# Attention with a low-rank mixer on one core: k transposed first in the first pair, and uT of the fourth pair in two PSUM banks

## The chip, the cores and the metric

One core of a Trainium2 chip. The metric is the device time of one execution in microseconds. A run of a program on one core is called slow when it is over 1.5% above the fastest of the same kernel. The granted clock is the share of full speed that TensorE was given in a stretch. PSUM is the memory in which this kernel keeps the tiles that TensorE writes its products to, SBUF that of the tiles it reads them from. By a bank is meant here a part of 512 columns of the kernel's PSUM tiles: an accumulator tile has one, a score tile two. The span of a profile is some 1.8 us shorter than the time of the same execution: 408.0 us of span went with 409.81 us of time.

## The reference, cut to what matters

Eight batches of attention with 8 heads, 576 positions and 64 channels per head, with a bias by relative position, and behind it a mixer: a low-rank product over the positions (U, V) is added to x, which gives u, and u goes through two dense layers (w1, w2).

```python
scores = scale * np.matmul(q, k.transpose(0, 1, 3, 2)) + bias      # softmax, times v -> x
xt = x.transpose(0, 2, 1)
h = xt @ U @ V
u = x + h.transpose(0, 2, 1)
ch = np.maximum(u @ w_ch1, 0.0) @ w_ch2
return u + ch
```

## The kernel before: the parts that matter here

Heads are handled in pairs; batch 0 has pairs 0 to 3, numbered on through the batches. The first pair's q and k are transposed on TensorE into two PSUM tiles; VectorE copies q's, ScalarE copies k's:

```python
def first_transposes(pr, srcs, copies):          # pr = 0: srcs = (q, k), copies = (vector, scalar)
    # ... tv[0], tv[1]: one PSUM tile each
    for ti, src in enumerate(srcs):
        for t in range(4):
            if pr == 0:
                nc.tensor.transpose(tv[ti][:, t], src[:, t * 128 : (t + 1) * 128], ident)
            # ...
    for ti in range(2):
        copies[ti](out=qkT[0][:, pr, ti, 0:S0]..., in_=tv[ti]...)
```

u transposed (uT) is what w1 is multiplied with. For the pairs of batch 0 TensorE makes it, in one PSUM tile of the pool `acc` (three tiles of one bank); tt is the low-rank part, copied to SBUF by ScalarE just before:

```python
def mix_ut(g, copy):
    tp = acc()
    nc.tensor.matmul(tp, lhsT=tt, rhs=vpad[:, 0:S0], start=True, stop=False, ...)
    for t in range(4):
        nc.tensor.matmul(tp[:, t * 128 : (t + 1) * 128], lhsT=x[:, t, :], rhs=ident, ...)
    copy(uT[b % 3][:, pr, :], tp)

# ... at the end of batch 0's attention
mix_t(3, nc.scalar.copy)                 # tt of the fourth pair
mix_ut(3, nc.vector.tensor_copy)         # uT of the fourth pair; the first w1 products follow
```

The scores come from another pool, `sc`, of two tiles with two banks each. GpSimd issues most loads on one queue. For batch 2 they come in this order, and TensorE transposes the four q tiles of pair 8 at about 70 us:

```python
for t in range(NKT):                     # NKT = 4
    for which in range(2):               # q, k
        seq.append(lambda which=which, t=t: main(which, t))
```

And at the start, GpSimd waits for the small bias table in DRAM (gp_dram) before it loads v of batch 0:

```python
nc.gpsimd.dma_start(out=gate, in_=gp_dram[0:1, 0:2])
load_rem(0, 2)                           # v, last 64 rows
for t in range(NKT):
    load_main(0, 2, t)                   # v, four tiles
```

The softmax here doesn't subtract the row's maximum and nothing guards it: scores larger than these inputs give would overflow.

## Time and profile before

| | before |
|---|---|
| median of the first three runs | 409.9 us (409.36 to 410.46) |
| span of the profile, mean granted clock | 408.0 us, 0.992 |
| first scores | 7.66 us |
| first uT product of the fourth pair | 38.13 us |
| first w1 product that needs it | 39.53 us |
| transpose of the fourth q tile of pair 8 | 70.68 us, after 1.30 us of waiting |

The chain of waits runs through loads up to the last row of the table and through TensorE from there on. The lines are in the prediction.

### The profile page before, as it was taken

What the parts mean: (1) busy time and instruction counts of PE and PEld (TensorE: products, weight loads), DVE (VectorE), ACT (ScalarE), POOL (GpSimd) and SP (SyncE); (2) the same over time, 40 slices, a digit from 0 to 9 for tenths busy, and PEclk for the clock granted to TensorE, in tenths of its full rate; (3) what the DMA queues carried; (4) which work ended last, traced back from release to release, by engine and by line L of the source; (5) the groups of instructions that cost most, each with busy time, mean ns of one, the idle gap of its engine ahead of it and who ended that gap; (6) DMA issues with size and microseconds to landing.
All of it is one profiled execution on the core that took longest, in us unless ns stands there. A gap on an engine that the chain in (4) does not pass through costs nothing.

```text
span 408.0 us, 9061 instructions
## 1 busy us (share of the span) xinstructions
PE 386.7 (95%) x3636; PEld 214.8 (53%) x3700; DVE 243.2 (60%) x554; ACT 207.0 (51%) x289; POOL 124.7 (31%) x179
## 2 busy tenths in 40 slices
PE   3888998999999999999999999999999999999995
PEld 1456555555555555555555555555555554444443
DVE  6867887757664675566755776568655832422321
ACT  5886644565654566557655665455555640220310
POOL 4948924454454045404540454040000000000000
PEclk9789999999999999999999999999999999999999
DMA  7999999999999599949995999499022003001012
GB/s 130 181 159 157 112 187 128 119 104 155 151 78 117 123 117 94 129 104 135 108 100 130 127 88 91 110 135 105 14 66 66 14 14 95 35 4 75 26 27 77
DMA packets 162754, 40.68 MB, mean 100 GB/s; under 512 B 151792, under 2 KB 157176, under 8 KB 162712
## 3 DMA queue, kind: packets, MB, share of 16 engines
q0 software_dynamic: 108416, 17.97, 62.2%
q1 hardware_dynamic: 53080, 21.22, 25.6%
q10 hardware_dynamic: 1216, 0.92, 0.7%
q8 instruction: 29, 0.48, 0.5%
q14 instruction: 13, 0.11, 0.1%
HBM read 37.84 MB, written 9.45 MB: 116 GB/s over the span
## 4 chain that ended last, share of the span: by engine, by line
PE 81%; DMA 10%; POOL 5%; issue 2%; DVE 1%; ACT 0%; ACTq 0%; POOLq 0%
PE acc L392 30%; PE acc L372 27%; PE o L611 10%; PE sc L524 7%; DMA w1b<-in_moe_w_ch_dram 5%; DMA w2b<-in_moe_w_ch_dram 4%; PE acc L647 2%; POOL v_bf L255 2%; POOL qb L265 1%; PE acc L663 1%; DMA qb<-in_q_dram 1%; PE sc L537 1%; PE sc L558 1%; POOL qb L255 1%; DMA gp_dram<-gp 1%
## 5 line engine op out<-in xcount | busy, mean ns | idle before, releaser
L533 ACT ACTIVATE p_sb<-sc 128x1024 bf16<-128x1024 f32 x128 | 124.6, 1021 | 101.3 <-PE sc L524 101.1
L392 PE MATMUL acc<-w2b,g 128*128 128x512 bf16 (+1 forms) x560 | 128.7, 373 | 2.3 <-DVE ob L401 0.5
L372 PE MATMUL acc<-uT,w1b 128*128 128x512 bf16 x484 | 116.3, 380 | 2.5 <-issue 0.6
L392 PEld LDWEIGHTS <-g 128*128 128x128 bf16 x592 | 55.2, 98 | 70.2 <-issue 11.7
L372 PEld LDWEIGHTS <-w1b 128*128 128x128 bf16 x576 | 53.3, 98 | 71.5 <-issue 13.1
L383 DVE TENSOR_SCALAR g<-acc 128x512 bf16<-128x512 f32 x94 | 64.7, 690 | 34.7 <-PE acc L372 31.7
L587 DVE TENSOR_TENSOR p_sb<-p_sb,eb 128x768 bf16<-128x768 bf16 (+3 forms) x160 | 69.8, 465 | 12.1 <-ACT p_sb L533 9.5
L381 ACT ACTIVATE g<-acc 128x512 bf16<-128x512 f32 x50 | 29.9, 598 | 59.8 <-PE acc L372 59.6
L611 PEld LDWEIGHTS <-p_sb 128*128 128x128 bf16 x1600 | 56.3, 98 | 6.9 <-issue 1.3
L611 PE MATMUL o<-v_bf,p_sb 128*128 128x65 bf16 x1500 | 58.3, 194 | 0.2 <-DVE p_sb L587 0.2
L401 DVE TENSOR_TENSOR ob<-acc,u_tok 128x512 f32<-128x512 f32 x32 | 22.1, 691 | 44.3 <-PE acc L392 39.4
L524 PE MATMUL sc<-qkT 64*128 64x512 bf16 x256 | 41.7, 395 | 1.3 <-ACT qkT L469 0.7
L914 POOL COPY gate<-xp 1x2 bf16<-1x2 bf16 x18 | 3.1, 175 | 121.7 <-DVE xp L636 121.7
L671 DVE TENSOR_TENSOR u_tok<-acc,xp 128x512 bf16<-128x512 f32 x32 | 22.1, 691 | 24.8 <-PE acc L663 24.7
L636 DVE TENSOR_TENSOR xp<-o,rcp 128x320 bf16<-128x320 f32 x60 | 29.5, 491 | 3.2
L255 POOL DMA_DIRECT2D v_bf<-in_v_dram x32 | 28.5, 915 | 2.0 <-DMA w1b<-in_moe_w_ch_dram 1.7
L255 POOL DMA_DIRECT2D qb<-in_q_dram x24 | 22.1, 921 | 5.0 <-DVE p_sb L587 5.0
L255 POOL DMA_DIRECT2D qb<-in_k_dram x24 | 21.9, 910 | 5.5 <-DMA w2b<-in_moe_w_ch_dram 3.5
L567 ACT ACTIVATE p_sb<-sc 128x640 bf16<-128x640 f32 x32 | 22.4, 698 | 0.4 <-PE sc L561 0.3
L550 ACT ACTIVATE p_sb<-sc 128x512 bf16<-128x512 f32 x32 | 19.1, 598 | 3.5 <-PE sc L537 1.2
L634 DVE RECIPROCAL rcp<-o 128x5 f32<-128x5 f32 x60 | 11.5, 191 | 14.0 <-PE o L611 13.3
L647 PEld LDWEIGHTS <-upad 128*128 128x128 bf16 x160 | 11.4, 98 | 7.8 <-DVE xp L636 0.7
(90 smaller groups left out, 257.5 us busy)
## 6 DMA issues: line engine op xcount, KB each, us to landing
out_dram<-ob SPq DMA_DIRECT2D x32, 256.0 KB, 2.3
v_bf<-in_v_dram POOLq DMA_DIRECT2D x32, 128.0 KB, 5.7
qb<-in_q_dram POOLq DMA_DIRECT2D x27, 128.0 KB, 4.4
qb<-in_k_dram POOLq DMA_DIRECT2D x27, 128.0 KB, 4.5
w1b<-in_moe_w_ch_dram POOLq DMA_DIRECT2D x2, 1024.0 KB, 9.3
w2b<-in_moe_w_ch_dram POOLq DMA_DIRECT2D x2, 1024.0 KB, 12.5
stage<-gp_dram SPq DMA_DIRECT2D x4, 192.0 KB, 4.6
qkT<-qb SPq DMA_TRANSPOSE x40, 5.0
```

The lines of the kernel that those rows point to most:

```text
L255: nc.gpsimd.dma_start(out=dst, in_=src[b, :, t * 128 : (t + 1) * 128, :].rearrange("h p d -> p h d"),)
L372: nc.tensor.matmul(gp_, lhsT=w1b[:, ct, nt * 128 : (nt + 1) * 128], rhs=rhs[:, ct, :], start=(ct == 0), stop=(ct == 3),)
L381: nc.scalar.activation(g[:, nt, :], gp_, AF.Relu)
L383: nc.vector.tensor_relu(out=g[:, nt, :], in_=gp_)
L392: nc.tensor.matmul(op[:, c0:c1], lhsT=g[:, nt, tt * 128 : (tt + 1) * 128], rhs=w2b[:, nt, c0:c1], start=(nt == 0), stop=(nt == NHT - 1), s ...
L401: nc.vector.tensor_tensor(out=ob[:, c0:c1].rearrange("p (a c) -> p a c", c=128), in0=op[:, c0:c1].rearrange("p (a c) -> p a c", c=128), in ...
L524: nc.tensor.matmul(sp[:, hh, :], lhsT=kT[rows, i * 128 : (i + 1) * 128], rhs=qT[rows, 0:S0], start=True, stop=True,)
L533: nc.scalar.activation(P[:, i, :, 0:S0], sp, AF.Exp, scale=scale)
L567: nc.scalar.activation(P4[:, 0:SP], sp.rearrange("p a c -> p (a c)")[:, 0:SP], AF.Exp, scale=scale,)
L587: nc.vector.tensor_tensor(out=t, in0=t, in1=e, op=ALU.mult)
L611: nc.tensor.matmul(o[:, qt * 66 : qt * 66 + 65], lhsT=lhs[:, c0 : c0 + 128], rhs=rhs, start=(kt == NKT and qt == 0), stop=(kt == NKT - 1), ...
L636: nc.vector.tensor_tensor(out=xo[:, :, hh], in0=o[:, :, 0:64], in1=rbc, op=ALU.mult)
```

## The change

The intent: let k be transposed as soon as it is cast, since ScalarE casts it before q, and copy uT of the fourth pair with two engines side by side from two banks, since TensorE waits 0.29 us for that copy.

```diff
-        for ti, src in enumerate(srcs):
+        for ti in (1, 0) if pr == 0 else (0, 1):
+            src = srcs[ti]
             for t in range(4):
...
-        for ti in range(2):
+        for ti in (1, 0) if pr == 0 else (0, 1):
             copies[ti](
...
     mix_t(3, nc.scalar.copy)
-    mix_ut(3, nc.vector.tensor_copy)
+    x, tt = x_pr[3], tt_pr[3]
+    sc = ps_s.tile([128, 2, 512], FP32, name="sc")
+    for w, copy in enumerate((nc.scalar.copy, nc.vector.tensor_copy)):
+        cols = slice(w * 256, (w + 1) * 256)
+        nc.tensor.matmul(sc[:, w, 0:256], lhsT=tt, rhs=vpad[:, cols], start=True, ...)
+        for t in range(2):
+            nc.tensor.matmul(sc[:, w, t * 128 : (t + 1) * 128], lhsT=x[:, 2 * w + t, :], rhs=ident, ...)
+        copy(uT[0][:, 3, cols], sc[:, w, 0:256])
```

(The arguments of the two products are shortened.)

More of the change, by code (lines that the diff above doesn't have):

```diff
@@ L889 @@
     mix_t(3, nc.scalar.copy)
-    mix_ut(3, nc.vector.tensor_copy)
+    x, tt = x_pr[3], tt_pr[3]
+    sc = ps_s.tile([128, 2, 512], FP32, name="sc")
+    for w, copy in enumerate((nc.scalar.copy, nc.vector.tensor_copy)):
+        cols = slice(w * 256, (w + 1) * 256)
+        nc.tensor.matmul(
+            sc[:, w, 0:256], lhsT=tt, rhs=vpad[:, cols], start=True, stop=False,
+            skip_group_check=True,
+        )
+        for t in range(2):
+            nc.tensor.matmul(
+                sc[:, w, t * 128 : (t + 1) * 128],
+                lhsT=x[:, 2 * w + t, :],
+                rhs=ident,
+                start=False,
+                stop=(t == 1),
+                skip_group_check=True,
+            )
+        copy(uT[0][:, 3, cols], sc[:, w, 0:256])
     put_off = [lambda g=g: mix_h(g) for g in range(NPAIR)]
```

## The prediction

> **What bounds the kernel now.** I read four views, in this order: the page's chain of work that ended last, the same chain cut to the first 75 us, the waits of TensorE up to 75 us, and the timeline around the two places that the change touches. The page says TensorE: busy 95% of the span, and 81% of the chain. But the change lies in the first 40 us, so what matters is what carries the chain there. That is another thing:
>
> ```profile
> PE 386.7 (95%) x3636; PEld 214.8 (53%) x3700; DVE 243.2 (60%) x554; ACT 207.0 (51%) x289; POOL 124.7 (31%) x179
> PE 81%; DMA 10%; POOL 5%; issue 2%; DVE 1%; ACT 0%; ACTq 0%; POOLq 0%
> ```
>
> ```profile
> 17.48 10.41 DMA w1b<-in_moe_w_ch_dram
> ...
> 29.68 8.12 DMA w1b<-in_moe_w_ch_dram
> ...
> 47.67 14.56 DMA w2b<-in_moe_w_ch_dram
> 62.24 0.30 issue
> 62.54 2.59 POOL qb L255 x3
> 65.13 5.50 DMA qb<-in_q_dram
> 70.63 0.05 issue
> 70.68 0.29 PE acc L498 x2
> ```
>
> The columns are start, duration, what. Up to 70.63 us the chain runs through GpSimd's queue of loads: two halves of w1, two of w2, then the q tiles of batch 2. Only at 70.68 does it pass to TensorE, and from there it stays on it (127.5 us busy of the 129 between 71 and 200). The waits of TensorE before 75 us show the joint between the two:
>
> ```profile
> PE acc L459 <- ACT qb L237: 5.9, 1, 5.9
> PE acc L498 <- DMA qb<-in_q_dram: 1.3, 1, 1.3
> ...
> PE sc L524 <- ACT qkT L469: 0.7, 1, 0.7
> ...
> PE acc L372 <- DVE uT L704: 0.3, 1, 0.3
> ```
>
> (total, times, longest, in us.) The second row is the joint: TensorE reaches the transpose of the fourth q tile of batch 2 about 1.3 us before the tile has landed. The two other waits are the ones that the change goes for: 0.7 us for the second copy of the first pair's transposes, and 0.3 us for uT of the fourth pair. The timeline there:
>
> ```profile
> 5.95 1.03 PE L459 MATMUL acc<-ident,qb 128*128 128x128 bf16 x8 [5.95 <-ACT qb L237]
> 6.59 0.69 DVE L469 COPY qkT<-acc 128x512 bf16<-128x512 bf16 x1 [0.53 <-PE acc L459]
> 7.02 0.58 ACT L469 COPY qkT<-acc 128x512 bf16<-128x512 bf16 x1 [1.13 <-PE acc L459]
> 7.66 1.03 PE L524 MATMUL sc<-qkT 64*128 64x512 bf16 x4 [0.68 <-ACT qkT L469]
> ...
> 38.13 0.39 PE L691 MATMUL acc<-vpad,tt 128*128 128x512 bf16 x1 [0.36 <-ACT tt L655]
> 38.36 0.39 PE L696 MATMUL acc<-ident,xp 128*128 128x128 bf16 x4
> 38.79 0.69 DVE L704 CAST uT<-acc 128x512 bf16<-128x512 f32 x1 [1.54 <-PE acc L696]
> 38.81 0.38 PE L558 MATMUL sc<-qkT 128*128 128x512 bf16 x1
> 39.53 1.89 PE L372 MATMUL acc<-uT,w1b 128*128 128x512 bf16 x8 [0.29 <-DVE uT L704]
> ```
>
> The reader is to see that the first scores wait for ScalarE's copy (7.02 + 0.58), not for VectorE's (6.59 + 0.69), and that the first product that needs all of uT starts 0.05 us after VectorE's cast ends at 39.48.
>
> [...] the row of the load at 65.13 is 0.90 us long, its data is awaited until 70.63. So a load that looks short can bound TensorE for 5.5 us.
>
> **Part one, k first.** ScalarE casts k before q, two casts of 0.67 us from 4.56, so k is ready at 5.23 and q at 5.90. Today the transposes of q come first and those of k lie behind them. After the change the four of k can begin at about 5.28 (5.23 plus the 0.05 that passed between 5.90 and 5.95). Eight transposes took 1.03 us, four of them about 0.5, so k is in PSUM at some 5.85, before q's transposes can begin at 5.95. ScalarE, free at 5.90, copies k from about 5.95 to 6.55 (0.58 us). The q transposes begin at 5.95 as before, VectorE's copy runs from 6.59 to 7.28 as before. The scores then wait for VectorE and start at about 7.34 instead of 7.66: 0.32 us sooner. ScalarE's exponentials, which run without a gap from 8.31 for 3.90 us, start sooner by as much, and so does what follows.
>
> **Part two, uT in two banks.** The instruction count is small: one product of 512 columns becomes two of 256, the four products of 128 columns stay, one weight load is added, one copy of 512 elements (0.69 us on VectorE) becomes one of 256 on ScalarE and one of 256 on VectorE. Costs from the trace: ScalarE takes 0.27 us for 128 elements and 0.585 for 512 (rows of tt and uT), so 256 take 0.37; VectorE takes 0.69 for 512 at 1.04 ns each, so 256 take 0.42.
> The intent is that both copies run side by side. The listing of the built program's instructions with their waits says otherwise. The two halves are one PSUM tile, and waits are kept by tile: the second half's first product waits for the ScalarE tick that the first half's copy gives (43, where tt gave 42), and VectorE's copy waits for it too. So the halves run one after the other. Besides, the new tile comes from the scores' pool of two: the score product of 512 columns that follows (L558 of before) now reuses that very tile and waits for VectorE's copy. Worked out on the old clock:
> - First half begins at 38.13; 0.12 (half of the 0.23 between the rows at 38.13 and 38.36) and 0.06 later its last product begins, at 38.31. The reader starts 0.26 after that begin (38.53 to 38.79 today, the 38.53 being 38.36 plus three steps of 0.056): ScalarE copies from 38.57 to 38.94.
> - Second half from 38.99 (0.05, as from tt to its reader), its last product at 39.17, VectorE's copy from 39.43 to 39.85.
> - L558's product from 39.90 instead of 38.81; the next after 0.21 and the w1 product after 0.06 more: 40.17 instead of 39.53.
> Sum of part two: 0.64 us later. Sum of both at this place: 0.64 - 0.32 = about 0.3 us later than before, if part one's gain lasts until there. If it is eaten by a load on the way, 0.6.
>
> **What it makes of the end.** Between 39.5 and 70.7 TensorE is nearly full (28.27 busy of the 29.4 us from 40.0 to 69.4), so it would carry 0.3 to 0.6 us to the wait for the q tile and reach it at about 69.7 to 70.0 instead of 69.4. The tile lands when GpSimd's queue has got that far. In the listing that queue waits, from the w2 loads to this tile, for its own earlier loads (the row at 62.54 waited 3.5 us for w2), for buffers free since long, and for two gates that need results of VectorE at 37.2 and 54.7 us, used at 48.5 and 58.9. None is within 0.6 us of mattering. So the tile still lands at 70.6 and the wait shrinks from 1.3 to 0.7 to 1.0. After it TensorE's order is the same, instruction by instruction, in the listing: same end.
>
> **The rivals.**
> - The intended gain comes through: 0.3 from part one and about 0.3 from part two, 409.3 us. For it speaks only that both waits are real in the profile. Against it: the tile-wise wait, the reused score tile, and the wait at 70.68, which would swallow it.
> - The loss of part two comes through: 410.2 to 410.5 us. It needs the q tile to land with TensorE's progress. The transposing loads that VectorE triggers on the other queue do move with it (one starts at 59.92)[...].
> - It is hidden by the load: 409.9 us. The chain of waits and TensorE's 1.3 us at 70.68 speak for it. This is my prediction.
> - A large effect, by the changed turn of the score or accumulator tiles afterwards: the listing shows equal waits from there on apart from one dropped, so I give it very little.
>
> **Range and chances.** The predicted time is 409.9 us. Three runs of before spread from 409.36 to 410.46, more than any of the rivals moves it, so the range is that spread with a little added: 409.2 to 410.6. A change of 2% would be 8.2 us, more than ten times each term: faster 0.01, same 0.98, slower 0.01.
>
> **What would show each step right or wrong.** Right: ScalarE's copy of k before VectorE's of q and the first scores near 7.34; ScalarE's half copy ending before the second half's first product begins; the 512-column score product waiting about 0.5 us for VectorE's half copy; the w1 product 0.3 to 0.6 us later than 39.53; the wait for the q tile at 70.6 shorter by that, with the tile landing within 0.2 us of before. Wrong would be: two half copies that overlap in time (then I misread the waits), a landing of the q tile that moved by as much as TensorE (then the queue of loads follows compute), or a TensorE that reaches the tile after it has landed (then a loss comes through to the end).

## The result, and the profile after

The changed kernel took 410.41 us in the median of six runs (408.98 to 411.31), the kernel before 410.12 us in six (408.77 to 410.46). The ratio is the mean time of one kernel's fast runs over that of the other's of the same rounds, so not quite the ratio of these medians: 1.0012, with a 95% interval from 0.9989 to 1.0035. The median lies half a microsecond above the forecast, near the upper edge of its range, and the first profile shows that the forecast's main step did not hold in it. From the page of the changed kernel, the granted clock in 40 slices and the chain that ended last:

```profile
PEclk9969999999999999999999999999999999999999
...
PE 84%; DMA 8%; POOL 5%; issue 1%; DVE 1%; ACT 0%; ACTq 0%; POOLq 0%
```

TensorE's share of the chain is up from 81 to 84%. In this kernel the chain passes from a load (the remainder rows of batch 2) to TensorE at 61.3 us already, and there is no wait at the q tile. The third slice (20 to 31 us) ran at 0.6 of the clock (a digit is cut to tenths). Now the first pair, in the timeline (start, duration, instruction):

```profile
5.86 0.58 ACT L470 COPY qkT<-acc 128x512 bf16<-128x512 bf16 x1
...
6.55 0.69 DVE L470 COPY qkT<-acc 128x512 bf16<-128x512 bf16 x1 [0.49 <-PE acc L460]
...
7.30 1.04 PE L525 MATMUL sc<-qkT 64*128 64x512 bf16 x4 [0.78 <-DVE qkT L470]
```

As predicted, ScalarE's copy of k now comes first, the scores wait for VectorE, and they start 0.36 us sooner (7.30 against 7.66). The fourth pair's uT:

```profile
39.52 0.28 PE L895 MATMUL sc<-vpad,tt 128*128 128x256 bf16 x1 [0.36 <-ACT tt L656]
...
39.95 0.37 ACT L908 CAST uT<-sc 128x256 bf16<-128x256 f32 x1 [0.49 <-PE sc L900]
40.38 0.27 PE L895 MATMUL sc<-vpad,tt 128*128 128x256 bf16 x1 [0.46 <-ACT uT L908]
...
40.87 0.42 DVE L908 CAST uT<-sc 128x256 bf16<-128x256 f32 x1 [2.23 <-PE sc L900]
...
41.34 0.38 PE L559 MATMUL sc<-qkT 128*128 128x512 bf16 x1 [0.36 <-DVE uT L908]
...
41.61 1.89 PE L372 MATMUL acc<-uT,w1b 128*128 128x512 bf16 x8
```

The two copies do not overlap: the second half's first product waits for ScalarE's copy (in the brackets: 0.46 us, released by ScalarE's uT), and the score product waits for VectorE's. From the first uT product to the w1 product it takes 41.61 - 39.52 = 2.09 us, against 39.53 - 38.13 = 1.40 before. That is the 0.64 us of the prediction, measured as 0.69.

What was not predicted is that all this lies 1.4 us later than before, in spite of the earlier start: the first uT product comes at 39.52 instead of 38.13. In between, pair 0's products with v wait twice. Two lines of TensorE's timeline in the changed kernel:

```profile
18.38 0.24 PE L612 MATMUL o<-v_bf,p_sb 128*128 128x65 bf16 x2 [1.07 <-DVE p_sb L588]
...
20.45 0.43 PE L612 MATMUL o<-v_bf,p_sb 128*128 128x65 bf16 x5 [0.78 <-DMA v_bf<-in_v_dram]
```

And around 20 us the clock goes to half. In stretches of one microsecond (columns: length, then busy time and count of TensorE, its weight loads, VectorE, ScalarE, GpSimd; then granted clock, DMA share, GB/s):

```profile
19.00:20.00 1.00, 0.67 (x17) 0.46 (x14) 1.00 (x4) 0.70 (x2) 1.00 (x2) 1.00 2.01 206
20.00:21.00 1.00, 0.55 (x10) 0.55 (x10) 0.54 (x2) 0.00 (x0) 1.00 (x3) 0.53 1.46 239
...
27.00:28.00 1.00, 1.00 (x27) 0.72 (x24) 0.00 (x0) 0.25 (x1) 0.00 (x0) 1.00 2.14 148
```

In the microsecond from 19 us TensorE was busy for 0.67 us, and its longest idle stretch between 15 and 20.5 us was the 1.07 us above. The kernel before had as much half speed in its first profile (6.83 us of it, against 6.82), but earlier. The same view over two longer stretches, first of before, then of the changed kernel (the granted clock is the third number from the end):

```profile
15.00:23.00 8.00, 7.06 (x80) 4.48 (x80) 6.49 (x16) 6.65 (x13) 7.91 (x12) 0.57 1.65 203
23.00:38.00 15.00, 13.24 (x234) 9.41 (x230) 10.20 (x27) 12.60 (x19) 8.31 (x12) 1.00 1.20 149
```

```profile
15.00:23.00 8.00, 5.19 (x67) 3.43 (x64) 6.78 (x15) 5.37 (x11) 7.65 (x12) 0.82 1.71 202
23.00:38.00 15.00, 13.98 (x232) 10.13 (x232) 10.85 (x27) 11.87 (x18) 9.35 (x13) 0.87 1.24 157
```

With the w1 product at 41.61 us (39.52 + 2.09), TensorE came to the q tile of pair 8 when the tile had landed. The line of the four transposes has no wait behind it; the fourth starts at 71.31:

```profile
71.15 0.39 PE L499 MATMUL acc<-ident,qb 128*128 128x128 bf16 x4
```

### The profile page after: what moved, and what is told of

Read it like the earlier page. It is cut to its first block, busy times and chain, and to the rows that moved or that the text cites. A ratio compares the mean times of both kernels' runs of the same rounds, so it can differ in the third digit from the quotient of the medians.

```text
span 408.7 us, 9130 instructions
## 1 busy us (share of the span) xinstructions
PE 391.4 (96%) x3701; PEld 215.5 (53%) x3701; DVE 243.8 (60%) x554; ACT 207.3 (51%) x290; POOL 124.9 (31%) x179
## 3 DMA queue, kind: packets, MB, share of 16 engines
q0 software_dynamic: 108416, 17.97, 61.3%
## 4 chain that ended last, share of the span: by engine, by line
PE 84%; DMA 8%; POOL 5%; issue 1%; DVE 1%; ACT 0%; ACTq 0%; POOLq 0%
PE acc L392 31%; PE acc L372 28%; PE o L612 10%; PE sc L525 7%; DMA w1b<-in_moe_w_ch_dram 4%; DMA rem<-in_k_dram 3%; PE acc L648 2%; PE acc L664 2%; POOL qb L265 2%; POOL v_bf L255 2%; PE sc L538 1%; PE sc L559 1%; PE acc L499 1%; DMA gp_dram<-gp 1%; POOL eb L213 1%
## 5 line engine op out<-in xcount | busy, mean ns | idle before, releaser
L392 PE MATMUL acc<-w2b,g 128*128 128x512 bf16 (+1 forms) x592 | 133.0, 374 | 0.5 <-DVE ob L401 0.5
L372 PE MATMUL acc<-uT,w1b 128*128 128x512 bf16 x512 | 119.6, 380 | 0.2 <-ACT uT L705 0.2
L588 DVE TENSOR_TENSOR p_sb<-p_sb,eb 128x768 bf16<-128x768 bf16 (+3 forms) x160 | 70.3, 467 | 10.8 <-ACT p_sb L534 10.3
```

What stands on the lines that cost most here:

```text
L372: nc.tensor.matmul(gp_, lhsT=w1b[:, ct, nt * 128 : (nt + 1) * 128], rhs=rhs[:, ct, :], start=(ct == 0), stop=(ct == 3),)
L392: nc.tensor.matmul(op[:, c0:c1], lhsT=g[:, nt, tt * 128 : (tt + 1) * 128], rhs=w2b[:, nt, c0:c1], start=(nt == 0), stop=(nt == NHT - 1), s ...
L588: nc.vector.tensor_tensor(out=t, in0=t, in1=e, op=ALU.mult)
```

## The experiments

Two theories. The first is the prediction's, with the joint made sharp: the end is a constant after the transpose of the fourth q tile, and that transpose starts at the later of two times, the tile's landing and TensorE's arrival; what TensorE wins or loses before is hidden as long as the tile comes last. The rival: the change costs or wins its 0.3 to 0.7 us at the end, whatever the tile does. A second question is where part one's 0.36 us went.

### One part at a time, and a control

`again` is the kernel before, unchanged. 

> The kernel before, unchanged, run as a control. Both theories: ratio 1.000 within 0.2%. What it tells apart is in the trace: if the arrival of the 8 KB table in DRAM (2.6 us in the first profile of before, 3.1 in that of the changed kernel) and the start of GpSimd's queue behind it (9.2 against 9.8 us) are chance, this run's may lie anywhere from 9.2 to 9.9 us, and TensorE's first uT product of the fourth pair anywhere from 38.1 to 39.5 us. If they belong to the change, this run repeats 9.2 and 38.1 within 0.1 us, with a wait of 1.3 us for the q tile of batch 2.

Measured: ratio 1.001 (0.9992 to 1.0028), for the same program as its partner: differences of 0.1% between two kernels of six runs are noise here. In the trace GpSimd's queue started at 9.78 us, not 9.23, and the first uT product came at 38.48, the wait at the q tile was 0.99 us. So the later table is chance. The kernel before did not come as late as the 39.5 us of the changed one.

`k_first` is part one alone. 

> Part one alone. First scores at 7.3 us instead of 7.66 in both theories. Theory hidden by the load: from the first uT product of the fourth pair to the first w1 product that needs it 1.40 us as before, TensorE at the q tile of batch 2 about 0.35 us sooner, the wait there longer by that, end as before within 0.1%. Rival, the early start collides: VectorE's two copies of the remainder bias slow down (0.75 and 0.36 us before, 1.04 and 1.13 with the change) and TensorE gets to the fourth pair no sooner or even later than 38.1 us.

```diff
-        for ti, src in enumerate(srcs):
+        for ti in (1, 0) if pr == 0 else (0, 1):
+            src = srcs[ti]
```

(and the same for the copies). Measured: 0.9993 (0.9975 to 1.0011). The first scores came at 7.74 us only, since the cast of q was late in this run (its transposes began at 6.36), the first uT product at 39.02, that is no sooner than in the kernels without it, and the interval to the w1 product was 1.40. The wait at the q tile was 0.31 us and not longer: the number expected for it was wrong, the gain had gone before. The rival of the expectation came true in its outcome (no sooner at the fourth pair). Whether by its cause is not separated: VectorE's two copies of the remainder bias took 0.75 and 0.72 us here, but together 0.94 to 2.17 us over all traces with k first and 0.93 to 1.44 without.

`split_only` is part two alone. 

> Part two alone. First scores at 7.66 us as before. From the first uT product of the fourth pair to the first w1 product that needs it 2.1 us instead of 1.40 in both theories (one after the other). Theory hidden by the load: TensorE still waits about 0.6 us for the q tile of batch 2 and the end is that of before within 0.1%. Rival, the loss comes through: no wait at the q tile, end later by 0.3 to 0.7 us.

Its edit is the second half of the diff. Measured: 1.0002 (0.9985 to 1.0018). First uT product at 38.39, interval 2.09 us, and TensorE still waited 0.90 us at the tile, which landed late (the transpose started at 71.22). So the 0.69 us are part two's alone, and here they were hidden.

`two_tiles` has both parts, but each half has a tile of its own. 

> Both parts, but the two halves of uT in two separate accumulator tiles instead of the halves of one score tile. If the tile-wise wait and the reused score tile are what made part two slow, the two copies now overlap in time and the interval from the first uT product of the fourth pair to the first w1 product that needs it is 1.15 us (before 1.40, changed 2.09). If it were the two engines' reading or the smaller instructions, it stays near 2. End: as before within 0.1% if hidden by the load, sooner by 0.5 us if not.

```diff
-    sc = ps_s.tile([128, 2, 512], FP32, name="sc")
+    halves = [acc(), acc()]
...
-        copy(uT[0][:, 3, cols], sc[:, w, 0:256])
+        copy(uT[0][:, 3, cols], halves[w][:, 0:256])
```

Its timeline:

```profile
40.76 0.28 PE L895 MATMUL acc<-vpad,tt 128*128 128x256 bf16 x1 [0.36 <-ACT tt L656]
...
41.19 0.37 ACT L908 CAST uT<-acc 128x256 bf16<-128x256 f32 x1 [0.49 <-PE acc L900]
...
41.41 0.42 DVE L908 CAST uT<-acc 128x256 bf16<-128x256 f32 x1 [1.55 <-PE acc L900]
...
41.89 1.47 PE L372 MATMUL acc<-uT,w1b 128*128 128x512 bf16 x6
```

The same instructions with the same durations, and now the copies overlap (41.41 lies inside 41.19 + 0.37): the interval is 1.13 us, less than the 1.40 of before. That settles what made part two slow: not the two engines, not the smaller pieces, but the wait that goes by tile, and the score tile that the next score product had to wait for (the two together, this run does not part them). The time was 1.0008 (0.9989 to 1.0027) all the same. In this profile the first uT product came at 40.76 us, with 10.24 us of half speed from 19.2 us on; what the other five runs did is not seen.

### Taking the wait at the q tile away

For these, q of batch 2 is loaded ahead of k:

```diff
-        for t in range(NKT):
-            for which in range(2):
-                seq.append(lambda which=which, t=t: main(which, t))
+        order = [(t, which) for t in range(NKT) for which in range(2)]
+        if b == 2:
+            order.sort(key=lambda p: p[1])
+        for t, which in order:
+            seq.append(lambda which=which, t=t: main(which, t))
```

`before_q` is the kernel before with this edit. 

> The kernel before, with the four q tiles of batch 2 loaded ahead of its four k tiles, so that the fourth q tile leaves GpSimd's queue three places sooner. In the six traces so far the span is 337.3 us plus the start of the transpose of that tile, and that start is the later of two: the tile's landing (70.6 to 71.2) and 29.8 us after the first w1 product that needs uT of the fourth pair. Theory joint: with the tile gone from the comparison TensorE does not wait there, the transpose starts at 69.4 to 69.7 and the span falls by 1.0 to 1.3 us against before, 0.3%. Rival, the queue follows compute or another load takes its place (the k tiles, 3 us later): span as before.

Measured: 0.9972 (0.9953 to 0.9991), median 408.2 us. TensorE transposes the four tiles without a wait:

```profile
68.78 0.39 PE L500 MATMUL acc<-ident,qb 128*128 128x128 bf16 x4
```

The fourth of them starts three steps of 0.056 us later, at 68.95, and 408.0 - 70.68 = 337.3 us before is 406.3 - 68.95 = 337.3 here. The joint holds, and the wait for the tile was worth 1.2 us of the end.

`after_q` is the changed kernel with it. 

> The changed kernel with the same reordered loads. Theory joint: TensorE does not wait at the tile in this kernel anyway (71.3 us), so the reordering changes little, and the changed kernel ends later than the reordered kernel before by what it is late at the w1 product: 0.7 us for the halves one after the other, plus what the earlier start loses at the loads of v (0 to 1.4 us). Rival, the change's cost is hidden or chance: both reordered kernels end alike within 0.2 us.

Measured: 0.9993 (0.9976 to 1.0009). The mean of six runs was 409.35 us, that of the reordered kernel before 408.43: the change costs 0.9 us where nothing hides it.

`two_only_q` has the two accumulator tiles without k first. 

> The kernel before with the halves of uT in two accumulator tiles (k not first) and the reordered loads. From the first uT product of the fourth pair to the first w1 product that needs it 1.13 us, as in the run with both parts, against 1.40 in the kernel before: 0.27 us sooner at the tile than the reordered kernel before, and the same at the end if the joint theory holds: about 1.4 us under before in all. Rival: the gain is lost on the way, span equal to that of the reordered kernel before.

Measured: 0.9986 (0.9967 to 1.0004), interval 1.13 us. The end was not sooner than that of `before_q`; in the profile a half-speed window (3.41 us) lay from 25 to 29 us and the first uT product came at 39.97. The gain of 0.27 us is there at its place and did not show at the end.

`after_again` is the changed kernel once more. 

> The changed kernel once more, as a control of its first profile. Theory: the early start is lost where pair 0's products wait for the third tile of v, and in the kernels with k first TensorE is idle there for longer, after which the clock stays at half until 25 us or later (23.2 or sooner in the three traces without k first). So: a wait of 0.7 us or more for v at about 20 us, half clock until 25 us or later, first uT product of the fourth pair after 39.0 us. Rival, the clock's phase is chance: it may as well come at 38.1 to 38.5 us as in the kernels without k first.

Measured: 1.0005 (0.9981 to 1.0029). This fell out for the rival: the clock never went to half, the first uT product came at 38.34, and TensorE did wait at the tile:

```profile
70.78 0.23 PE L499 MATMUL acc<-ident,qb 128*128 128x128 bf16 x1 [0.52 <-DMA qb<-in_q_dram]
```

So half speed until 25 us is no fixed consequence of k first. (Over all traces the half-speed windows number 1.1 per trace with k first and without. When they come is another matter, see the sorting below.)

### Taking the wait for v away

For these, on the base with the q tiles first, v is loaded ahead of the wait for the bias table:

```diff
-    nc.gpsimd.dma_start(out=gate, in_=gp_dram[0:1, 0:2])
     load_rem(0, 2)
     for t in range(NKT):
         load_main(0, 2, t)
+    nc.gpsimd.dma_start(out=gate, in_=gp_dram[0:1, 0:2])
```

`before_qv`: the kernel before. 

> The kernel before with the q tiles of batch 2 first and, further, the loads of v of batch 0 issued ahead of GpSimd's wait for the bias table instead of behind it (from about 4.4 us instead of 9.8). In the ten traces so far the first remainder score of the third pair comes 11.2 to 11.8 us after GpSimd's queue starts on v, and in most of them pair 0's products wait 0.6 to 1.3 us for a tile of v. Theory pinned: with v there early that wait is gone, the score comes sooner than 20.7 us, and the end with it, about 0.5 us under the reordered kernel before. Rival: the bias tiles or the earlier traffic of the loads take its place and nothing is won.

`k_first_qv`: part one. 

> Part one alone on the same base (q tiles first, v early), to be compared with that base. Theory pinned: with nothing to wait for at v, the 0.36 us by which the first scores start sooner last to the first uT product of the fourth pair and to the end: 0.3 to 0.4 us sooner than the base if the clock is at full speed in both, or an equal number of half-speed windows. Rival: the bias products on VectorE or the exponentials pin it, and the gain is gone by 21 us again.

`two_tiles_qv`: both parts, separate tiles. 

> Both parts on the same base, with the halves of uT in two accumulator tiles. Interval from the first uT product of the fourth pair to the w1 product 1.13 us. If both gains last, 0.27 plus 0.36 us sooner than the base, and about 2 us under the kernel before; this is then the fastest version. Rival: as for the run before.

`after_qv`: the change as it is. 

> The change as it is, on the same base. Neither the wait for the q tile nor that for v is there to hide or to eat anything, so it shows the bare sum of the prediction: 0.69 later by part two, 0.36 sooner by part one, 0.3 us later than the base at the w1 product, and the same at the end, with an equal number of half-speed windows. Rival: the ends are equal, or the change is faster.

Measured: 1.0028 (1.0013 to 1.0043), 0.9999 (0.9981 to 1.0017), 0.9985 (0.9959 to 1.001) and 1.002 (0.9993 to 1.0046). The rival held: no wait for v was left, but the bias tiles took its place. GpSimd now gets the table at 10.5 to 10.8 us instead of 9.2 to 9.9 (10.35 in `k_first`), and waits again for the tiles made of it; from `before_qv`:

```profile
15.57 1.03 POOL L213 COPY eb<-stage 128x768 bf16<-128x768 bf16 x1 [4.23 <-DMA stage<-gp_dram]
```

The third pair's first remainder score came at 20.1 to 20.8 us, little sooner than before, with up to 3.0 us of waits for the bias products (in `k_first_qv`), and single runs scattered from 407.3 to 412.4 us. The means of six were 410.32, 409.48, 408.87 and 410.31 us, with standard errors of 0.33 to 0.59. So part one and both parts in separate tiles ended 0.84 and 1.45 us under this base, in the order that was expected but by over twice as much, and the change as it is ended level with it. The base itself was 1.9 us slower than with the q tiles first alone (408.43), and the one trace of part one had its first uT product at 40.20 us against 38.51 in the base. These ends are no clean measure of the parts.

### The parts on the base with the q tiles first

`before_q2`: that base again. 

> The kernel before with the q tiles of batch 2 first, a second time, as the base of the three that follow. Theory: about 408.4 us as in the six runs of the first time, 0.3% under before, TensorE not waiting at the q tile. Rival: the first time was luck, and it ends as before within 0.1%.

`k_first_q`: part one on it. 

> Part one alone on the base with the q tiles first. Theory: the 0.36 us are eaten at the loads of v, so this ends as the base, within 0.3 us, in runs with the same number of half-speed windows of the clock; the first remainder score of the third pair comes 11.2 to 11.8 us after GpSimd's queue starts on v, as in all traces. Rival: the gain lasts, 0.36 us under the base.

`two_tiles_q`: both parts, separate tiles. 

> Both parts on the base with the q tiles first, the halves of uT in two accumulator tiles. Interval from the first uT product of the fourth pair to the w1 product that needs it 1.13 us against 1.40. Theory: 0.27 us under the base at that place and, within the noise, at the end; the change's intent needs other tiles and a base without the wait at the q tile. Rival: no difference at the end that the noise lets show.

`after_q2`: the change as it is. 

> The change as it is on the base with the q tiles first, a second time. Theory: 0.69 us later than the base at the w1 product, and about as much later at the end (the first time 409.35 against 408.43 us in the mean of six). Rival: the ends are equal within 0.2 us, and the first time was noise.

| on the base with the q tiles first | ratio to before, 95% | mean of six runs | first uT product, interval to w1 |
|---|---|---|---|
| before_q2 | 0.9976 (0.9962 to 0.9990) | 408.47 | 37.97, 1.39 |
| k_first_q | 0.9983 (0.9967 to 0.9999) | 408.66 | 37.79, 1.40 |
| two_tiles_q | 0.9989 (0.9974 to 1.0004) | 409.05 | 38.42, 1.14 |
| after_q2 | 1.0004 (0.9981 to 1.0027) | 409.66 | 38.29, 2.09 |

With both times together (12 runs each) the change ends at 409.50 us and its base at 408.45, 1.05 us apart (standard error 0.29); 0.69 of it is the interval, the rest is within what the runs of one kernel scatter. Part one wins nothing that the ends show. The separate tiles win 0.26 us at their place and nothing that the ends show.

### Sorting the runs by the clock

`after_third` and `before_third` are both kernels as they are. 

> The changed kernel a third time, for its runs sorted by the mean clock (1.000, 0.996, 0.992: none, one or two half-speed windows of 3.4 us). Theory: the change uses up most of the slack at the q tile, so runs without such a window end as before (409.5 us) and runs with two end near 410.5 us, as in the first twelve runs (409.45, 409.58, 410.6 for none, one, two). Rival: no dependence, 410.1 us throughout, or none at all, 409.6 us.

 

> The kernel before in the same rounds. Theory: its slack of 1.0 to 1.3 us at the q tile takes up a late TensorE, so its end does not depend on the number of half-speed windows (409.49, 409.53, 409.73 us for none, one, two in 33 runs beside the experiments). Rival: it depends as that of the changed kernel does.

Measured: 1.0002 (0.9979 to 1.0026) and 1.0006 (0.9985 to 1.0027). Of the 20 traces, 15 have a stretch at half speed: it lasts 3.41 or 3.42 us in nine, 6.82 or 6.83 in five and 10.24 in one. So it is counted here in windows of 3.41 us. By estimate each takes 0.5 x 3.41 / 408 = 0.0042 from the mean clock, and the number of windows of a run is read from its mean clock, rounded; in all 20 traces that number is the one seen in the trace. All runs of both kernels beside the first six of before, by that number (mean time in us, runs in brackets):

| half-speed windows | none | one | two | three |
|---|---|---|---|---|
| before (68 runs) | 409.56 (19) | 409.81 (27) | 409.59 (22) | |
| changed (18 runs) | 409.19 (5) | 409.75 (6) | 410.63 (6) | 412.20 (1) |

By this count the kernel before does not depend on the windows and the changed one does. Over all, 409.67 us (standard error 0.08) against 410.02 (0.23): about 0.35 us, 1.4 times its error. Round by round the changed kernel's mean was 0.48, 0.26 and 0.11 us over its partner's. The sorting is of runs as they fell, no experiment set the clock.

That the wait at the tile makes the kernel before independent of the windows is not shown. On the base without that wait the same sorting gives 408.43 us (5 runs), 408.07 (2), 408.59 (4) and 408.74 (1) for none to three windows in `before_q` and `before_q2`: no dependence there either. With the change on that base it gives 409.29 (5), 409.31 (4), 409.22 (2) and 411.91 (1).

The traces sort better by when the half speed comes than by how often. Eight of the 20 have 2.2 to 6.5 us of it after 23 us, and their first uT product of the fourth pair comes at 38.51 to 40.76 us, 39.64 in the mean. The other twelve have at most 0.5 us of it there, seven of them with one or two windows before, and theirs comes at 37.35 to 38.78, 38.11 in the mean. (The 23 us were chosen from these same traces.) Of the nine traces with the old loads, four of the five with k first are among the eight and none of the four without; of all, six of twelve and two of eight. Whether k first moves the half speed is open.

## Why the prediction was right or wrong

**Within 2%: right, but not by the path forecast.** The median of the six runs, 410.41 us, came out 0.5 us above the forecast; whether a part of that is real stays open. The step that was to keep the end at 409.9, the wait for the q tile, failed (see below). The range of the forecast held the ends of all three small rivals, 409.3 to 410.5 us, so the end of one comparison could not tell them apart.

**Part two, one half after the other: right.** Predicted 0.64 us later, measured 0.69 in every one of the seven traces that have it (2.09 against 1.39 or 1.40). ScalarE's 256 elements took 0.372 us (predicted 0.37), VectorE's 0.425 (0.42), where 512 took 0.585 and 0.692 in the kernel before. The 1.04 ns per element that the prediction used for VectorE is in the profile of the kernel before as well: its writes to `ob` from `acc` took 691 ns for 512 elements and 424 for 256. The prediction rested on the listing, and `two_tiles` agrees: with separate tiles the same instructions take 1.13 us.

**Part one's 0.32 us: right at its place (0.36), wrong as far as it was to last to the fourth pair.** The prediction said "if part one's gain lasts until there", with 0.6 in the other case; the other case came. In the 16 traces without the early v loads, the first scores come at 7.52 us in the mean with k first (nine traces) and at 7.91 without (seven), but the third pair's first remainder score at 21.20 and 21.08: the gain is gone by then. Counted from the start of GpSimd's queue, that score comes at 11.50 and 11.55 us. TensorE, sooner at pair 0's products with v, waits there for a tile of v or for the bias products, both of which come through that queue (0.2 to 1.3 us at v in all but four of these traces). Most of the gain is lost earlier still: VectorE's first product with the bias starts at 16.97 us in the mean with k first and at 17.06 without. That this queue sets both fits the traces, but is not shown: taking one of its two waits away put the other in its place, so the pair was not separated.

**The wait for the q tile "shrinks from 1.3 to 0.7 to 1.0. After it ... same end": this step failed.** The mechanism is right: in all 20 traces the span is 337.3 to 337.4 us plus the start of that transpose, whether TensorE waited (before, `again`, `k_first`, `split_only`, `after_again`, `before_third`) or not. With the tile loaded sooner the end of the kernel before fell by 0.28 and 0.24% in the two times it was tried. In the 14 traces without a wait the transpose comes 29.67 to 29.70 us after the w1 product. So what was mis-sized is the term before that: TensorE's arrival. The prediction took the first uT product at 38.13 from one profile, moved it by the sum of the parts, and had TensorE at the tile at 69.7 to 70.0 us. In the three profiles of the changed kernel the first uT product came at 39.52, 38.34 and 39.42 us, TensorE arrived at 71.31, about 70.1 and 71.19, and the wait was 0, 0.52 and 0 us instead of 0.7 to 1.0. In three profiles of the kernel before, that product came at 37.35 to 38.48, so the scatter of one program is about as large as the slack of 1.0 to 1.3 us. The tile scatters too: in the six traces with a wait at it the transpose starts at 69.76 to 71.22, at 69.76 and 70.70 in the two repeats of the kernel before. The forecast of 70.6 for the changed kernel held roughly (70.78 in `after_again`).

Three things moved the arrival. The 0.69 us of part two are measured. Part one's 0.36 us did not last, where the sum of 0.3 us counted on it. The third goes with the clock, which falls to half at some time from 15 to 36 us for none to three windows of 3.4 us (0 to 10.24 us in all): both late profiles of the changed kernel have 3.9 us of half speed after 23 us, and the one at 38.34 and the three of before have at most 0.3 us there. By estimate 3.9 us at half speed are 1.9 us of work lost if TensorE had work throughout. This agreement is of traces as they fell; no experiment set the clock, and what sets it stays open.

**The rival "the loss of part two comes through"** was described with a wrong condition: the tile need not follow TensorE's progress; it is enough that TensorE is later than the tile. The criterion given at the end of the prediction ("a TensorE that reaches the tile after it has landed") named the right sign.

**Rivals of the intended gain and of a large effect**: both rightly given little.

What stays open: how much of the 0.35 us is real (the intervals include 1), what makes the clock fall in one run and not in another, and early in one and late in another, whether k first has a part in it, and whether the 0.27 us of the separate tiles would reach the end of a kernel with less scatter.

The version that beats both kernels is not the change: the kernel before with the q tiles of batch 2 loaded ahead of the k tiles, 408.2 and 408.56 us in the median, 0.9972 and 0.9976 of before, with both intervals under 1. The two waits of the intent were real, but neither was what held the end.

## What to carry to other kernels

A wait that hides a loss has a size, and one profile gives one draw of it: take a second and third profile of the same program before calling a half microsecond hidden. Two banks of one tile gave two engines nothing here, since the framework keeps its waits by tile (2.09 us with both halves in one tile, 1.13 with a tile each, from another pool besides, against 1.40 before): look at the waits of the built program, and give each half its own tile from a pool that nobody waits for next. And where TensorE waits for a load, ask first for another order of the loads: it was a few lines here, and of all that was tried it alone ended clearly under the kernel before in both tries.
